# Rows of 320 columns, a tile for the gate matrix, and the later steps' gate sums spread over units 0 to 5

## The chip, the cores and the metric

The kernel runs on one core of one Trainium2 chip. The metric is device time in microseconds of one execution.

## The reference

Three layers follow one another, all in float32.

```python
# 1. attention: 4 x 8 heads, 768 steps, head size 40
for t in range(S):
    m_new = np.maximum(f_gate[:, :, t] + m, i_gate[:, :, t])
    f_stab = np.exp(f_gate[:, :, t] + m - m_new)
    i_stab = np.exp(i_gate[:, :, t] - m_new)
    m = m_new
    C = f_stab * C + i_stab * einsum('bhd,bhe->bhde', vt, kt)
    n = f_stab * n + i_stab * kt
    h_tilde = einsum('bhde,bhe->bhd', C, qt)
    denom = np.maximum(np.abs(einsum('bhd,bhd->bh', n, qt)), 1.0)
    y[:, :, t] = sigmoid(o_gate[:, :, t]) * h_tilde / denom
# 2. experts: 3072 tokens of 320; (token, expert) pairs taken in order of their logit,
#    each expert takes at most 384 tokens, each token one expert
logits = x @ w_gate                       # 8 experts
out[mask_e] = np.maximum(x[mask_e] @ w1[e], 0.0) @ w2[e]      # 320 -> 1024 -> 320
# 3. one dense layer for all tokens
h = x @ w_in                              # 320 -> 2048
out = np.where(h > 0, h, np.exp(np.minimum(h, 0)) - 1) @ w_out
```

## The kernel before

**Attention** (`Attention`) cuts the 768 steps into 12 blocks of 64. A unit u holds block u // 2 and one of two pairs of batches, with eight heads in two halves of the partitions, so there are 24 units, and `run` goes through them in order. All instructions stand in the order in which the Python issues them; each engine's queue, and that of each DMA issuer, takes them in that order.

Ahead of the units the gates are summed up over time, for all 32 (batch, head) pairs at once on 32 partitions: `maximum` is the running m (L227, a scan on DVE), `logs` turns the gates into sums (L236 to L242: two subtractions or additions, a scan, two more), and `split` cuts each sum into three bfloat16 parts `fp` and `pb` (ACT copies at L251 and L252, DVE subtractions at L254 and L255) and copies `pb` twice into `fb` (L258). For the first 128 steps all of it is done in the setup. For the 640 others `maximum` and `logs` are issued in the setup as one piece each, and `split` in three pieces in units 0, 1 and 2, each behind the unit's first matmuls and ahead of `decay`.

A unit u issues, in this order: a warm-up matmul (`idle`, L351); `values(u)` (weights P times v, L360) mixed with `scores(u + 2)` (L292); `decay(u + 2)`, which builds the decay factors with matmuls on `fp` and `fb` (L307 to L317) and takes exponentials on ACT into `db` (L305) and W (L312); `turn(u - 1)`, three transposes of the finished rows x (L431) and a copy on ACT into xT (L433); in units 5, 9, 13, 17 and 21 `tokens`, a transpose of collected logits (L453); `recall(u)` and `state(u)` (L374, L387); `factors` and `fade` on POOL (qt L324, kt L333, C L335); `weigh(u + 1)` on DVE, which writes P (L345); `load_qk(u + 5)` on SP; `opens` on ACT; `gates(u)`, a short chain on DVE (rd, L407 to L411) with the rows x at its end (DVE L414, POOL L415); `logits(u - 1)` (L443 or L445); `add_state` on DVE (L398); `rows_out(u)`; `load_vk(u + 4)` on SP. Between these, `fl` issues pieces of two other jobs: five pieces of the weights' conversion per unit from unit 2 on (a DMA into `cx`, ACT, three DVE operations L894, L898, L901 into cF, ACT `wih` L955, POOL `wil` L957), and tables for the router on DVE from unit 3 on.

A row x is 320 wide and its tile 384: `rows_out` copies columns 256 to 320 once more into 320 to 384 on ACT (L422) and then writes both halves on SP into `xd`, a table of 3072 rows of 384 in device memory. The duplicate serves the later matmuls, which take the last 64 columns twice, once on each half of the partitions. `wg`, the gate matrix, lies in columns 128 to 224 of the tile `keep`, whose first 32 partitions hold the scan's mask; its load is therefore issued on SP behind `logs` (L218).

**Routing and experts.** `Router.round(r)` picks the tokens of one expert at a time, on DVE and PE; `Mlp` does experts and dense layer in eight rounds of 384 tokens. `get_x` gathers a round's rows from `xd` with three indirect DMAs on POOL into `xg`; `prep_x` transposes them (L1078) and splits them into `xh` (ACT) and `xl` (DVE, L1086); `up` does the first products (L1125). In round 0 these steps follow at once; in later rounds a planner (`Plan`, which adds up estimated times by engine) decides when a side job such as `prep_xs` may issue its next instructions between the main matmuls: 5,000 ns of planned time behind `get_x`, and not before the round before is far enough.

Of the kernel before, what the change touches and what calls it, by code (L numbers as in the profile page):

```python
# [17 lines left out]
NS, NU = 12, 24  # L18
# [101 lines left out]
class Attention:  # L120
# [4 lines left out]
    def __init__(self, nc, tc, consts, qk, vk, ig, fg, wg, xd, L, ident):  # L125
        self.nc, self.tc, self.qk, self.vk, self.xd, self.L, self.ident = nc, tc, qk, vk, xd, L, ident
        self.es = ExitStack()
        one = self.es.enter_context(tc.tile_pool(name="a1", bufs=1))
        self.two = self.es.enter_context(tc.tile_pool(name="a2", bufs=2))
        self.psX = self.es.enter_context(tc.tile_pool(name="psX", bufs=1, space=PS))  # L130
        V, G, A = nc.vector, nc.gpsimd, nc.scalar
        self.st = {}
        self.extra = []
        gi = one.tile([32, S], F32, name="gi")
        gf = one.tile([32, S], F32, name="gf")
        nc.sync.dma_start(gf, fg)
        A.dma_start(gi, ig)
        junk = self.psum("pF", 1)
        wz = self.wz = one.tile([128, 512], BF, name="wz")
        V.memset(wz, 0.0)  # L140

        def spin(n):

            for _ in range(n):
                nc.tensor.matmul(junk, wz[:, :128], wz, start=True, stop=True)

        spin(SPIN)
        warm = one.tile([1, 8], F32, name="warm")
        V.memset(warm, 0.0)
        A.activation(warm, warm, AF.Tanh)  # L150
        self.QKb = [one.tile([128, 2, 8, 64], F32, name=f"qk{i}") for i in range(4)]
        self.QK, self.VK, self.W = {}, {}, {}
        for u in range(2):
            self.load_qk(u)
        for u in range(2):
            self.load_vk(u)
        for u in range(2, 4):
            self.load_qk(u)
        for u in range(2, 4):
            self.load_vk(u)  # L160
        m = one.tile([32, S + 1], F32, name="m")
        V.memset(m[:, 0:1], -1e30)
        keep = keep_all = one.tile([128, S], F32, name="keep")
        self.lT, keep = keep[:, :128], keep[:32]
        self.wg = keep_all[:, 128:224].rearrange("p (k e) -> p k e", e=32)
        G.memset(keep, 1.0)
        G.memset(keep[:, 0:S:64], 0.0)
        ac = one.tile([32, S], F32, name="ac")
        i3 = one.tile([96, 32], BF, name="i3")
        for k in range(3):  # L170
            V.tensor_copy(i3[k * 32:k * 32 + 32], ident[:32, :32])
        self.half = one.tile([96, 2], F32, name="half")
        V.tensor_reduce(self.half, i3.rearrange("p (r m) -> p r m", r=2), AX, ALU.max)
        pair = one.tile([96, 16], BF, name="pair")
        V.tensor_tensor(pair, i3[:, :16], i3[:, 16:], op=ALU.add)
        self.sel = one.tile([96, 16, 2, 64], BF, name="sel")
        V.tensor_copy(self.sel, i3.rearrange("p (r m) -> p m r", r=2)[:, :, :, None].to_broadcast([96, 16, 2, 64]))
        self.one_m = one.tile([96, 16, 64], BF, name="one_m")
        A.activation(self.one_m, pair[:, :, None].to_broadcast([96, 16, 64]), AF.Copy)
        self.idb = one.tile([128, 128], BF, name="idb")  # L180
        A.activation(self.idb, ident, AF.Copy)
        low = one.tile([128, 64], BF, name="low")
        G.memset(low, 0.0)
        for r in (0, 64):
            G.affine_select(out=low[r:r + 64], in_=low[r:r + 64], pattern=[[1, 64]], compare_op=ALU.is_ge, fill=-1e30,
                            base=0, channel_multiplier=-1)
        self.low = one.tile([128, 8, 64], BF, name="low8")
        A.activation(self.low, low[:, None].to_broadcast([128, 8, 64]), AF.Copy)
        self.fp = one.tile([96, S], BF, name="fp")
        self.pb = one.tile([96, S], BF, name="pb")  # L190
        self.fb = one.tile([96, NS, 2, 64], BF, name="fb")
        self.CS = [[one.tile([128, 8, 64], F32, name=f"C{b}{i}") for i in range(3)] for b in range(2)]
        for x in self.CS[0] + self.CS[1]:
            G.memset(x[:, :, 41:], 0.0)
        self.KT = [one.tile([128, 512 + 64 - D], F32, name=f"kt{i}") for i in range(2)]
        for x in self.KT:
            G.memset(x, 0.0)
        self.pC = self.psum("pC", 1)
        self.pX = self.psum("pX", 1).rearrange("p h t -> p (h t)")
        self.g = gi, gf, m, keep, ac  # L200

        t0, t1 = slice(0, 128), slice(128, S)
        self.maximum(0, 128)
        self.logs(0, 2)
        for _ in self.split(0, 2):
            pass
        self.opens(0)
        self.both(self.scores(0))
        self.load_qk(4)
        self.decay(0)  # L210
        self.maximum(128, S)
        V.memset(self.pC, 0.0)
        self.decay(1)
        self.both(self.scores(1))
        self.weigh(0)
        self.fade(0)
        self.logs(2, NS)
        nc.sync.dma_start(self.wg, wg)  # L218

    def psum(self, name, bufs):  # L220
        return self.psX.tile([128, 8, 64], F32, name=name, bufs=bufs)
# [6 lines left out]
                                              op1=ALU.max)  # L228

    def logs(self, n0, n1):  # L230

        gi, gf, m, keep, ac = self.g
        V = self.nc.vector
        a, b = n0 * 64, n1 * 64
        t = slice(a, b)
        V.tensor_tensor(gf[:, t], gf[:, t], m[:, t], op=ALU.add)  # L236
        V.tensor_tensor(gf[:, t], gf[:, t], m[:, a + 1:b + 1], op=ALU.subtract)
        if n0 == 0:
            V.memset(gf[:, 0:1], 0.0)
        V.tensor_tensor_scan(ac[:, t], keep[:, t], gf[:, t], 0.0, op0=ALU.mult, op1=ALU.add)  # L240
        V.tensor_tensor(gi[:, t], gi[:, t], m[:, a + 1:b + 1], op=ALU.subtract)
        V.tensor_tensor(gi[:, t], gi[:, t], ac[:, t], op=ALU.subtract)  # L242

    def split(self, n0, n1):

# [156 lines left out]
    def gates(self, u, fl):  # L402

        V = self.nc.vector
        nq = self.st["O", u][:, :, 40]
        rd = self.two.tile([128, 2, 8], F32, name="rd")
        V.tensor_scalar(rd[:, 0], nq, -2.0, 2.0, op0=ALU.mult, op1=ALU.max)  # L407
        fl(1)
        V.scalar_tensor_tensor(rd[:, 0], nq, 2.0, rd[:, 0], op0=ALU.mult, op1=ALU.max)
        fl(5)  # L410
        V.reciprocal(rd[:, 1], rd[:, 0])  # L411
        x = self.st["x", u] = self.two.tile([128, 384], F32, name="x", bufs=3)
        xh = x[:, :320].rearrange("p (h d) -> p h d", d=40)
        V.scalar_tensor_tensor(xh, self.st.pop(("sg", u)), 1.0, self.st.pop(("O", u))[:, :, :40], op0=ALU.add, op1=ALU.mult)  # L414
        self.nc.gpsimd.tensor_tensor(xh, xh, rd[:, 1, :, None].to_broadcast([128, 8, 40]), op=ALU.mult)  # L415

    def rows_out(self, u):
# [1 line left out]
        nc = self.nc  # L419
        n, bp = divmod(u, 2)  # L420
        x = self.st["x", u]
        nc.scalar.activation(x[:, 320:], x[:, 256:320], AF.Copy)  # L422
        for r in range(2):
            row = (bp * 2 + 1 - r) * S + n * 64
            nc.sync.dma_start(self.xd[row:row + 64], x[r * 64:r * 64 + 64])
# [1 line left out]
    def turn(self, u):  # L427
        x = self.st.pop(("x", u))
        p = self.pX
        for k in range(3):  # L430
            self.nc.tensor.transpose(p[:, k * 128:k * 128 + 128], x[:, k * 128:k * 128 + 128], self.ident)  # L431
        xT = self.st["xT", u] = self.two.tile([128, 3, 128], F32, name="xT")
        self.nc.scalar.activation(xT.rearrange("p k t -> p (k t)"), p[:, :384], AF.Copy)  # L433

# [24 lines left out]
            self.extra.pop(0)  # L459

    def run(self, hook, fill):
        later = self.split(2, NS)
        for u in range(NU):
            v, w = u + 1, u + 2
            fl = lambda i: ([fill() for _ in range(FP[i])] if u > FU else []) + [self.step() for _ in range(EP[i])]
            self.idle(u)
            self.both(self.values(u), self.scores(w))
            if u < 3:
                next(later, None)
            if w < NU:  # L470
                self.decay(w)
            if u > 0:
# [12 lines left out]
            if v < NU:  # L485
                self.fade(v)
            self.gates(u, fl)
            fl(2)
            if u > 0:
                self.logits(u - 1)  # L490
# [6 lines left out]
            if u + 4 < NU:  # L497
                self.load_vk(u + 4)
            fl(4)
            hook(u)  # L500
        self.turn(u)
        self.logits(u)
# [338 lines left out]
class Mlp:  # L841
# [209 lines left out]
    def get_x(self, r):  # L1051
        idx = self.router.res[r][1]
        self.xg = []
        for k in range(3):
            t = self.pool.tile([128, 384], F32, name="xg", bufs=3)
            self.xg.append(t)
            self.gather(t, self.xd, idx[:, k:k + 1])

    def psum(self):

# [3 lines left out]
    def spin(self, n):  # L1064

        for _ in range(n):
            self.nc.tensor.matmul(self.junk, self.wih[:, 0, :128], self.wih[:, 0, :512], start=True, stop=True)

    def prep_x(self, r):

        nc, plan = self.nc, self.plan
# [3 lines left out]

        def turn(k):
            for t in range(3):
                nc.tensor.transpose(ps[k][0][:, t * 128:t * 128 + 128], self.xg[k][:, t * 128:t * 128 + 128], self.ident)  # L1078

        def split(k):  # L1080
# [262 lines left out]
    def prep_xs(self):  # L1343

        for r in range(1, NR):
            while self.routed < r:
                yield self.plan.t + 1, ""
            self.get_x(r)
            yield self.plan.t + RX, ""
            while self.prog < r - 1:  # L1350
                yield self.plan.t + 1, ""
            yield from self.prep_x(r)
# [84 lines left out]
def kernel(ctx, tc, qk, vk, ig, fg, wg, w1a, w1b, w2a, win, wout, out):  # L1437
# [5 lines left out]
    ident = consts.tile([128, 128], F32, name="ident")  # L1443
    make_identity(nc, ident)
    L = consts.tile([128, 8, 24], F32, name="L")
    xd = dram.tile([3072, 384], F32, name="xd")
    rt = Router.__new__(Router)
    plan = Plan()
    m = Mlp(nc, tc, consts, w1a, w1b, w2a, win, wout, xd, out, ident, rt, plan)
# [98 lines left out]
```

## Time and profile before

| | |
|---|---|
| median of 3 runs | 772.03 us (771.68 to 773.65) |
| profiled execution: its own time, its span | 776.35 us, 774.5 us |
| busy, share of the span: PE, DVE, ACT, POOL | 92%, 70%, 49%, 28% |
| matmuls on PE | 7384 |
| instruction queue q8 | 58 packets, 0.95 MB |
| DMA in all | 68.89 MB, mean 89 GB/s |

PE is TensorE, DVE VectorE, ACT ScalarE, POOL GpSimd, SP the engine that issues most DMAs. A row of the timeline gives the start in us from the span's start, the duration in us, engine, line, operation, what it writes and reads, and in brackets how long the engine had sat idle and what ended that. "issue" there is a wait for nothing that the profile names.

### The profile page before, as it was taken

Reading aid. Unit: us, or ns where it says so; the run is one execution under the profiler, and the core shown is the slowest. Engines: PE = TensorE matmul, PEld = TensorE weight load, DVE = VectorE, ACT = ScalarE, POOL = GpSimd, SP = SyncE. Lnnn points to the kernel's source line nnn. Section 1 sums busy time; section 2 is a strip of 40 time slices with the busy share of each in tenths; the row PEclk is TensorE's granted clock in tenths of the full one; section 3 lists DMA queues with packets and bytes.
Section 4 is the critical chain, followed back from the end, with each engine's and each line's share of the span. In section 5 each row is a group of like instructions: output and inputs, shape, how many; then the busy total and the mean of one; then the engine's idle time right before and its main releaser. Section 6 shows DMA issues by size and latency. Waiting matters only on the chain.

```text
span 774.5 us, 18272 instructions
## 1 busy us (share of the span) xinstructions
PE 711.0 (92%) x7384; PEld 646.8 (84%) x7384; DVE 543.5 (70%) x1599; ACT 381.6 (49%) x807; POOL 214.9 (28%) x264
## 2 busy tenths in 40 slices
PE   7887887962899999999999999999999999999994
PEld 4565665651799998999999899999999999999994
DVE  8495867758878887885797589669768834842541
ACT  5654544523536644652574277246527734742542
POOL 5687866525401410401121030112023220001001
PEclk9898999885899999999999999999999999999998
DMA  7676867433500410410140032023003321100000
GB/s 258 198 248 193 244 199 222 134 88 105 177 2 2 146 60 1 125 57 27 33 148 20 7 104 78 26 83 99 1 26 111 127 79 36 36 1 25 1 1 26
DMA packets 22820, 68.89 MB, mean 89 GB/s; under 512 B 3536, under 2 KB 7632, under 8 KB 22736
## 3 DMA queue, kind: packets, MB, share of 16 engines
q1 hardware_dynamic: 14240, 35.91, 15.2%
q0 software_dynamic: 8448, 31.73, 12.3%
q8 instruction: 58, 0.95, 0.5%
q14 instruction: 26, 0.21, 0.1%
q10 hardware_dynamic: 48, 0.10, 0.0%
HBM read 59.06 MB, written 8.65 MB: 87 GB/s over the span
## 4 chain that ended last, share of the span: by engine, by line
PE 56%; issue 21%; DVE 8%; POOL 7%; ACT 3%; DMA 3%; SPq 0%; POOLq 0%; DVEq 0%; ACTq 0%
PE ph L1125 25%; PE acc L1264 5%; PE acc L1268 5%; PE acc L1265 5%; PE acc L1232 3%; PE acc L1233 2%; PE acc L1234 2%; POOL qt L324 2%; POOL kt L333 1%; PE acc L1219 1%; POOL x L415 1%; PE pO L374 1%; PE acc L1221 1%; POOL C L335 1%; DVE e L1178 1%
## 5 line engine op out<-in xcount | busy, mean ns | idle before, releaser
L1178 DVE SCALAR_TENSOR_TENSOR e<-e,ph 128x384 f32<-128x384 f32 x128 | 70.4, 551 | 54.7 <-ACT e L1175 54.0
L1174 ACT ACTIVATE e<-ph 128x384 f32<-128x384 f32 x128 | 62.4, 488 | 85.2 <-PE ph L1125 77.6
L1125 PE MATMUL ph<-yh,wih 128*128 128x384 f32 x256 | 89.9, 351 | 0.3
L1142 ACT ACTIVATE gh<-ph 128x384 fp32r<-128x384 f32 x64 | 31.4, 491 | 112.7 <-PE ph L1125 88.6
L1125 PE MATMUL ph<-yh,wil 128*128 128x384 f32 x256 | 86.6, 338 | 0.0
L1274 POOL DMA_INDIRECT out_dram<-ot,idx x24 | 24.1, 1004 | 210.1 <-ACT ot L1002 207.1
L1009 DVE TENSOR_TENSOR gl<-e,gh 128x384 fp32r<-128x384 f32 x128 | 71.1, 562 | 1.7 <-ACT gh L1002 0.3
L1175 ACT ACTIVATE e<-e 128x384 f32<-128x384 f32 x128 | 67.3, 526 | 4.0
L1264 PE MATMUL acc<-woh,gh 128*128 128x320 f32 x216 | 68.2, 316 | 0.0
L1149 DVE SCALAR_TENSOR_TENSOR gl<-ph,gh 128x384 fp32r<-128x384 f32 x64 | 35.3, 554 | 46.8 <-ACT gh L1142 46.4
L1265 PE MATMUL acc<-wol,gh 128*128 128x320 f32 x216 | 66.8, 309 | 0.0
L1268 PE MATMUL acc<-woh,gl 128*128 128x320 f32 x216 | 66.8, 309 | 0.0
L1125 PE MATMUL ph<-yl,wih 128*128 128x384 f32 x256 | 66.6, 342 | 0.0
L1013 POOL DMA_INDIRECT stg<-in_w1a_dram,wi x16 | 15.7, 982 | 148.4 <-DVE wi L782 134.1
L1002 ACT ACTIVATE gh<-e 128x384 fp32r<-128x384 f32 x97 | 49.4, 514 | 11.1 <-DVE e L1178 10.8
L1268 PE MATMUL acc<-woa,gl 128*128 128x320 f32 x168 | 52.4, 312 | 0.8 <-DVE gl L1009 0.8
L1264 PE MATMUL acc<-woa,gh 128*128 128x320 f32 x168 | 53.2, 316 | 0.0
L1265 PE MATMUL acc<-wob,gh 128*128 128x320 f32 x168 | 52.0, 309 | 0.0
L1125 PEld LDWEIGHTS ph<-yh,wih 128*128 128x128 f32 x256 | 48.3, 189 | 4.1 <-ACT yh L1237 4.1
L1125 PEld LDWEIGHTS ph<-yh,wil 128*128 128x128 f32 x256 | 48.2, 188 | 0.0
L1125 PEld LDWEIGHTS ph<-yl,wih 128*128 128x128 f32 x256 | 46.2, 188 | 0.0
L1125 PE MATMUL ph<-xh,w1h 128*128 128x384 f32 x128 | 44.9, 350 | 0.0
(275 smaller groups left out, 2096.6 us busy)
## 6 DMA issues: line engine op xcount, KB each, us to landing
vk<-in_vk_dram SPq DMA_DIRECT2D x24, 484.0 KB, 4.4
qk<-in_qk_dram SPq DMA_DIRECT2D x20, 320.0 KB, 5.0
xd<-x SPq DMA_DIRECT2D x48, 96.0 KB, 2.7
cx<-in_win_dram SPq DMA_DIRECT2D x8, 512.0 KB, 6.1
wx<-in_wout_dram SPq DMA_DIRECT2D x9, 320.0 KB, 3.0
cx<-in_wout_dram SPq DMA_DIRECT2D x5, 448.0 KB, 6.0
qk<-in_qk_dram SPq DMA_DIRECT2D x4, 512.0 KB, 6.7
cx<-in_win_dram SPq DMA_DIRECT2D x4, 256.0 KB, 6.0
```

Of the source, the lines that this page charges most:

```text
L1002: self.nc.scalar.activation(out, x, AF.Copy)
L1009: self.nc.vector.tensor_tensor(out, x, y, op=ALU.subtract)
L1125: PE.matmul(p, w, x, start=k == 0, stop=k == 7)
L1142: nc.scalar.activation(h, p, AF.Relu)
L1149: nc.vector.scalar_tensor_tensor(l, p, 0.0, h, op0=ALU.max, op1=ALU.subtract)
L1174: nc.scalar.activation(e, p, AF.Relu, scale=-1.0)
L1175: nc.scalar.activation(e, e, AF.Exp, scale=-1.0)
L1178: nc.vector.scalar_tensor_tensor(e, e, -1.0, p, op0=ALU.add, op1=ALU.max)
L1264: PE.matmul(p, h[:, c], wh, start=f == 0, stop=False)
L1265: PE.matmul(p, h[:, c], wl, start=False, stop=False)
L1268: PE.matmul(p, l[:, c], wh, start=False, stop=f == 15)
L1274: s = nc.gpsimd.indirect_dma_start(out=self.out, out_offset=bass.IndirectOffsetOnAxis(ap=idx[:, t:t + 1], axis=0), in_=o, in_offset=None)
```

## The change

Four things change. The rows are 320 wide in the tile x and in `xd`; the copy of the last 64 columns leaves `rows_out` and is made in the second part by `twice`, three times a round, on ACT, behind the gather; the third transpose in `turn` takes 64 columns, and pX is cleared once. The gate matrix has its own tile and is loaded early. `maximum` and `logs` for the later steps are done in two parts, steps 128 to 256 and 256 to 768, by `behind`, a generator whose next piece is issued twice a unit: behind `gates` and at the unit's end. `split` goes with it, so its pieces no longer stand ahead of `decay`. Counted out, unit 0 gets `logs(2, 4)` and the first piece of `split(2, 4)`, unit 1 the rest of it, unit 2 `maximum(256, S)` and the first two operations of the sums, unit 3 the scan and the last two, unit 4 two pieces of `split(4, NS)` and unit 5 the last.

```diff
         for u in range(2, 4):
             self.load_qk(u)
+        self.wg = one.tile([128, 3, 32], F32, name="wg")
+        nc.sync.dma_start(self.wg, wg)
         for u in range(2, 4):
             self.load_vk(u)
...
-        self.wg = keep_all[:, 128:224].rearrange("p (k e) -> p k e", e=32)
...
-        self.maximum(128, S)
+        self.maximum(128, 256)
         V.memset(self.pC, 0.0)
+        V.memset(self.pX, 0.0)
...
-        self.logs(2, NS)
-        nc.sync.dma_start(self.wg, wg)
...
+    def behind(self):
+        self.logs(2, 4)
+        yield
+        yield from self.split(2, 4)
+        yield
+        self.maximum(256, S)
+        yield
+        yield from self.steps(4, NS)
+        yield from self.split(4, NS)
+
+    def steps(self, n0, n1):
...
         V.tensor_tensor(gf[:, t], gf[:, t], m[:, t], op=ALU.add)
         V.tensor_tensor(gf[:, t], gf[:, t], m[:, a + 1:b + 1], op=ALU.subtract)
+        yield
...
         V.tensor_tensor_scan(ac[:, t], keep[:, t], gf[:, t], 0.0, op0=ALU.mult, op1=ALU.add)
+        yield
         V.tensor_tensor(gi[:, t], gi[:, t], m[:, a + 1:b + 1], op=ALU.subtract)
         V.tensor_tensor(gi[:, t], gi[:, t], ac[:, t], op=ALU.subtract)
+        yield
...
-        x = self.st["x", u] = self.two.tile([128, 384], F32, name="x", bufs=3)
+        x = self.st["x", u] = self.two.tile([128, 320], F32, name="x", bufs=3)
...
-        nc.scalar.activation(x[:, 320:], x[:, 256:320], AF.Copy)
...
-            self.nc.tensor.transpose(p[:, k * 128:k * 128 + 128], x[:, k * 128:k * 128 + 128], self.ident)
+            z = 128 if k < 2 else 64
+            self.nc.tensor.transpose(p[:z, k * 128:k * 128 + 128], x[:, k * 128:k * 128 + z], self.ident)
...
     def run(self, hook, fill):
-        later = self.split(2, NS)
+        later = self.behind()
...
-            if u < 3:
-                next(later, None)
...
             self.gates(u, fl)
+            next(later, None)
...
             fl(4)
+            next(later, None)
...
-            self.gather(t, self.xd, idx[:, k:k + 1])
+            self.gather(t[:, :320], self.xd, idx[:, k:k + 1])
...
+    def twice(self, k, ns=256):
+        self.nc.scalar.activation(self.xg[k][:, 320:], self.xg[k][:, 256:320], AF.Copy)
+        if ns:
+            self.plan.on("a", ns)
...
         def turn(k):
             for t in range(3):
+                if (r, t) == (0, 0):
+                    self.twice(k, 0)
...
             self.get_x(r)
             yield self.plan.t + RX, ""
+            for k in range(3):
+                self.twice(k)
+            yield self.plan.t, "a"
...
-    xd = dram.tile([3072, 384], F32, name="xd")
+    xd = dram.tile([3072, 320], F32, name="xd")
```

## Rows read from the trace of the kernel before

**Rows 1.** PE's busy tenths in 40 equal slices of the span.
```profile
PE   7887887962899999999999999999999999999994
```
**Rows 2.** Busy us by stretch: length, PE, PEld, DVE, ACT, POOL; clock, DMA, GB/s.
```profile
60.00:70.00 10.00, 6.50 (x132) 4.50 (x126) 5.12 (x11) 2.23 (x6) 6.16 (x7) 0.66 0.47 150
...
400.00:500.00 100.00, 99.95 (x681) 95.15 (x680) 76.42 (x249) 50.77 (x108) 14.27 (x19) 1.00 0.16 51
```
**Rows 3.** Timeline, PE: the warm-up matmuls of units 1 to 6.
```profile
16.52 0.39 PE L351 MATMUL pO<-wz 128*128 128x512 bf16 x1
...
23.70 0.39 PE L351 MATMUL pO<-wz 128*128 128x512 bf16 x1
...
32.99 0.61 PE L351 MATMUL pO<-wz 128*128 128x512 bf16 x1
...
38.40 0.39 PE L351 MATMUL pO<-wz 128*128 128x512 bf16 x1
...
45.39 0.39 PE L351 MATMUL pO<-wz 128*128 128x512 bf16 x1
...
51.19 0.39 PE L351 MATMUL pO<-wz 128*128 128x512 bf16 x1
```
**Rows 4.** Timeline, PE: two waits.
```profile
17.97 0.33 PE L360 MATMUL pO<-vk,P 64*64 64x64 f32 x3 [1.07 <-DVE P L345]
...
63.64 0.26 PE L387 MATMUL pC<-vk,kt 64*64 64x64 f32 x1 [3.50 <-issue]
```
**Rows 5.** Busy time by stretch, columns as in Rows 2.
```profile
20.00:37.50 17.50, 14.20 (x356) 10.51 (x351) 8.24 (x18) 11.46 (x23) 10.94 (x11) 0.80 0.67 195
37.50:57.50 20.00, 16.67 (x524) 12.16 (x519) 18.59 (x43) 10.43 (x24) 16.64 (x17) 1.00 0.80 249
```
**Rows 6.** Timeline, DVE: first and last of the sums, three waits, P.
```profile
10.29 0.91 DVE L236 TENSOR_TENSOR gf<-gf,m 32x640 f32<-32x640 f32 x1
...
14.31 1.36 DVE L242 TENSOR_TENSOR gi<-gi,ac 32x640 f32<-32x640 f32 x1
...
27.10 0.83 DVE L894 TENSOR_SCALAR cF<-cx 128x512 int32<-128x512 int32 x1 [1.86 <-DMA cx<-in_win_dram]
...
31.62 0.17 DVE L407 TENSOR_SCALAR rd<-pO 128x8 f32<-128x8 f32 x1 [3.68 <-PE pC L387]
...
37.69 0.17 DVE L407 TENSOR_SCALAR rd<-pO 128x8 f32<-128x8 f32 x1 [3.03 <-PE pC L387]
...
48.86 0.68 DVE L345 TENSOR_TENSOR P<-pS,W 128x512 f32<-128x512 f32 x1
```
**Rows 7.** A line's instructions: durations in ns least, median, most; first and last start; shapes.
```profile
L254 DVE TENSOR_TENSOR ac<-ac,fp x4: 279/546/823, 6.2 to 20.7; 32x128 f32<-32x128 f32 x2, 32x640 f32<-32x640 f32 x2
...
L227 DVE TENSOR_TENSOR_SCAN m<-gf,m,gi x2: 463/998/1533, 3.9 to 7.4; 32x128 f32<-32x128 f32 x1, 32x640 f32<-32x640 f32 x1
```
**Rows 8.** Timeline: POOL and DVE at work together.
```profile
20.78 1.32 POOL L333 TENSOR_TENSOR kt<-vk,W 128x320 f32<-128x320 f32 x1
...
21.60 1.17 DVE L255 TENSOR_TENSOR gi<-gi,pb 32x640 f32<-32x640 f32 x1
```
**Rows 9.** Timeline, ACT and PE in unit 21.
```profile
152.86 0.26 ACT L422 ACTIVATE x<-x 128x64 f32<-128x64 f32 x1 [1.25 <-POOL x L415]
...
154.53 0.33 PE L453 MATMUL pX<-ident,keep 128*128 128x128 f32 x1 [1.02 <-ACT xT L433]
```
**Rows 10.** Waits up to 168 us: total us, times, longest.
```profile
PE pX L453 <- ACT xT L433: 4.0, 5, 1.0
```
**Rows 11.** Timeline, PE: rounds 0 and 1 of the second part.
```profile
200.26 0.84 PE L1078 MATMUL ph<-ident,xg 128*128 128x128 f32 x3
...
275.38 0.62 PE L1125 MATMUL ph<-xl,w1h 128*128 128x384 f32 x2 [0.69 <-DVE xl L1086]
```
**Rows 12.** Busy time up to two of PE's pauses, columns as in Rows 2.
```profile
0.00:60.20 60.20, 49.00 (x1241) 34.92 (x1242) 46.53 (x101) 34.93 (x73) 41.33 (x71) 0.91 0.75 237
...
0.00:99.60 99.60, 80.96 (x2134) 58.28 (x2134) 74.45 (x158) 53.14 (x113) 71.52 (x99) 0.90 0.74 229
```

More of the change, by code (lines that the diff above doesn't have):

```diff
@@ L162, in __init__ @@
         V.memset(m[:, 0:1], -1e30)
-        keep = keep_all = one.tile([128, S], F32, name="keep")
+        keep = one.tile([128, S], F32, name="keep")
         self.lT, keep = keep[:, :128], keep[:32]
-        self.wg = keep_all[:, 128:224].rearrange("p (k e) -> p k e", e=32)
         G.memset(keep, 1.0)
@@ L230, in logs @@
     def logs(self, n0, n1):
+        for _ in self.steps(n0, n1):
+            pass
+    def behind(self):
[8 more added lines that the diff above has]
+    def steps(self, n0, n1):
         gi, gf, m, keep, ac = self.g
```

## The prediction

> **What bounds the kernel now.** I read first when PE is busy, then the busy shares by stage, and only then the waits, because an average hides two programs in one. PE is at nine tenths or more in every slice from about 213 us on but the last [rows 1], and busy 99.95 us of 100 between 400 and 500, at full clock [rows 2]: nothing there gets shorter unless matmuls are removed, and the change removes none. Ahead of that, up to 168 us, runs attention. Its slices stand at 7 to 9 tenths, and between 60 and 70 us PE is busy 6.50 us of ten at a clock of 0.66, with DMA at 0.47. The slice at 2 tenths behind it is the first routing round, a chain on DVE that the change leaves alone. Since PE is full later, each microsecond by which attention ends earlier is one of the whole, and the question is what attention's 24 units wait for.
>
> The start of each unit is its warm-up matmul [rows 3]. Unit 3 takes 38.40 - 32.99 = 5.41 us, which I use as the length of a unit that nothing holds up for long. Unit 1 takes 23.70 - 16.52 = 7.18 and unit 2 32.99 - 23.70 = 9.29. PE's own waits [rows 4] tell two kinds apart. In unit 1 it waits 1.07 us for P, a named piece of work. In unit 7, at 63.64, it waits 3.50 us for nothing that the profile names. At the start of unit 3 the warm-up takes 0.61 us where it takes 0.39 in others: TensorE is at 1.2 GHz there, after the stalls of unit 2.
>
> DVE is the other engine to read here [rows 5]: from 20 to 37.5 us it is busy 8.24 of 17.5, from 37.5 to 57.5 it is busy 18.59 of 20. So the idle time in units 1 and 2 sits directly in front of a stretch in which DVE is full.
>
> **The early units.** In the kernel before, the five DVE operations of the gates' sums over 640 columns run from 10.29 to 15.67 us in one piece [rows 6], and the split's first subtractions behind them, all ahead of P of unit 1: that is the 1.07 us. ACT's copies of 640 columns stand ahead of db, W and xT in units 1 and 2 in the same way. The change does 128 columns there, at 0.28 us an operation and 0.46 for the scan where 640 take 0.82 and 1.53 [rows 7], and moves the other 512 behind. Units 1 and 2 should then take about 5.4 each: 7.18 + 9.29 - 10.8 = 5.7 us earlier at the start of unit 3.
>
> **What the moved work costs where it goes.** Between the 128 and 640 columns of rows 7 I interpolate 512: 0.28 + 0.75 x 0.54 = 0.69 us for a two-input operation and 0.46 + 0.75 x 1.07 = 1.26 for a scan. Moved to units 2, 3 and 4 are two scans and eight two-input operations, 2.5 + 5.5 = 8.0 us. From the start of unit 2 to that of unit 5, 23.70 to 45.39 [rows 3], DVE idles 1.86 + 3.68 + 3.03 = 8.6 us [rows 6] and so works 13.1. Now unit 2 starts at 23.70 - 1.8 = 21.9, DVE owes 13.1 + 8.0 = 21.1, and the 1.86 us for the first weights' DMA remain: 44.9 us at the start of unit 5, against 45.39. If PE had to follow DVE closely, only 0.5 us of the 5.7 would be left. It needn't quite: P of unit 6 is ready at 48.86 + 0.68 = 49.54 [rows 6], and unit 6 starts at 51.19, so DVE may fall 1.65 us further behind before this holds PE. The lead that survives lies between 0.5 and 2.2 by that; I take 2.1, near the upper end, because the stalls of PE that gave DVE its idle time had PE at the low clock as well. The bounds are 0 and the whole 5.7.
>
> ACT's moved copies, in units 4 and 5, stand on an engine that is busy 10.43 of 20 us there [rows 5] and come at nothing; in a row without that cover, the last four can put an xT back by a microsecond. Clearing pX (DVE, 512 columns) comes ahead of the first P, in the microsecond that the shorter first scan gives back (1.53 against 0.46), and costs its half microsecond only without it.
>
> One row speaks against even that lead. At 21.60 a subtraction over 640 columns took 1.17 us beside a POOL operation of 1.32 us that runs up to 22.10 [rows 8]; that of rows 7 took 0.82 at most. The Trainium skill has a rule for it (GPSIMD Engine Reference, Key points): GpSimd shares its SBUF interfaces with VectorE and contends with instructions that read two SBUF inputs. By that rule the moved operations, nearly all with two SBUF inputs, come into a stretch in which POOL works 16.64 of 20 us [rows 5]. The trace agrees in this pair; were all 8.0 us stretched by 1.17/0.82, they would cost 3.4 us more, which is more than the lead that I leave, and this is what the first rival does.
>
> **The copy of 64 columns.** It leaves every unit, 24 times 0.26 us on ACT [rows 9]. What counts is its place: it waits for POOL's x, and db, W and xT stand behind it. That reaches PE only where PE wants xT at once, in units 5, 9, 13, 17 and 21, which transpose the logits' sums: 4.0 us of waits in 5 [rows 10]. In unit 21 ACT idles 1.25 us ahead of the copy, the copy ends at 153.12, db, W and xT take until PE goes on at 154.53, 0.47 each, and PE has waited 1.02 [rows 9]. Without the copy db would be done in that idle time: 0.5 us less. Five of those are 2.5; in the earlier units ACT also stands behind a DVE that is full, so I take 1.6 (bounds 0 and the 4.0). In other units the matmuls of recall and state, 64 between the transposes and the logits, hide xT; without them these would gain too.
>
> **Three copies a round in the second part.** In round 0 PE's last three transposes start at 200.26 as soon as the last gathered rows are there [rows 11], with the first product behind them; a copy of 0.26 us goes in between: +0.3 (bounds 0 and 0.8, all three). In round 1 PE waits 0.69 us for xl [rows 11]; three copies now go ahead of it on ACT, which may sit there until the third block of rows has landed: +0.4 (bounds 0 and 0.8). In later rounds matmuls of the round before are queued on PE, and I cost them at nothing; without that cover it would be 0.8 a round, 4.8 in six.
>
> **What I cost at nothing.** Rows of 1,280 instead of 1,536 bytes take 32 KB off a unit's writes, 0.13 us at 249 GB/s [rows 5], and these writes are read only after attention. The load of wg no longer holds SP's queue until DVE has done the sums; behind it there stood the keys of unit 5, wanted by unit 3, after 33 us. Now it stands ahead of the values of units 2 and 3, whose use also gets earlier, by its own issue alone; the bound is one issue, a few tenths. The third transpose still moves 128 columns.
>
> **The sum:** -2.1 - 1.6 + 0.3 + 0.4 = -3.0 us. The profiled execution took 776.35 us, its span being 774.5; that makes 773.35. The median shown is 4.3 lower, 772.03, and against it the forecast is 769.0. Under 0.3%, 2.3 us, a change can't be told from none, so this is just beyond it.
>
> **Rivals.** *Everything is given back on DVE* (the contention above, lead 0): what remains is -1.1 for the copies, since DVE then delays xT in the early ones, and +0.7: 771.6 us. For it speaks DVE's full stretch in rows 5; against it the 1.65 us of slack of P.
> *The lead is kept whole*, the moved operations fitting into waits of DVE such as it must have in PE's 3.50 us of unit 7: -5.7 - 1.6 + 0.7 = -6.6, 765.4 us. Against it: unit 7 comes after the full stretch.
> *Slower: more pauses of PE at its code.* The pause of 3.50 us comes after 1241 matmuls and another, at 99.6, after 2134 [rows 12]: 893 apart, 7 times 127.6. The execution's 7384 matmuls over the 58 packets of one instruction queue are 127.3 a packet. So PE seems to outrun its code while DMA engines are full. Earlier units mean denser loads, and so more or longer pauses. This decides from 5.3 us of added pauses on; two more of 3.50 make -3.0 + 7.0 = +4.0, 776.0 us. Against it: such pauses come in few of the units, and units 1 and 2 only get as fast as unit 3. (The Trainium skill, Runtime: NRT & Kernel Launch, Instruction fetch mechanics, has the crossing of such a block mostly hidden; by it this rival would cost nothing, and the trace, with its 3.50 us, does not agree.)
>
> **Numbers.** Forecast 0.46 (own range 767 to 771), given back 0.22, kept 0.16, slower 0.16. Of the forecast's chance two thirds, 0.30, lie beyond 0.3%, the rest within: faster 0.30 + 0.16 = 0.46, same 0.16 + 0.22 = 0.38, slower 0.16. The range, 764.5 to 774.5, takes in the first two rivals and stops short of the third's middle.
>
> **What would show it.** The profile after should have unit 3 start near 27 us, DVE full from about 25 us on, and the lead shrunk to 1 to 3 us by unit 6; the five waits for xT nearer 0.5 than 1 us; and the first product of the second part 0.3 us further behind the last gather. It would be wrong if the pauses at the code move: one more or one less is as large as the sum.

## The result, and the profile after

The changed kernel takes 778.48 us in the median of four runs (775.35 to 785.29), against 772.08 for the kernel before on the same chip (771.68 to 773.65): a ratio of 1.010, interval [1.0058, 1.0142]. A ratio here isn't the quotient of the two medians (that would be 1.008), and it leaves out runs of more than 1.5% above the fastest of their kernel. Forecast were 769.0 us with faster as the likeliest; it is slower, beyond the range of 764.5 to 774.5. The profiled execution of after is one of its short ones, 775.5 us with a span of 773.7, and that of before one of its long ones (776.35). So the two profiles, laid side by side, don't show the 6 us as a difference of spans. What they show is where the lead of the first units went.

First the page of after: busy tenths of PE and DVE in 40 slices of the span, and the granted clock of TensorE.

```profile
PE   7778787953999999999999999999999999999994
...
DVE  7898777868878877885797689569858834842541
...
PEclk9989999975899999999999999999999999999998
```

PE's row behind the routing round is that of [rows 1]: nothing has changed there. The stretches of [rows 5] and [rows 2] in the kernel after (length, PE, PEld, DVE, ACT, POOL; clock, DMA, GB/s):

```profile
20.00:37.50 17.50, 14.38 (x429) 10.63 (x425) 13.89 (x30) 8.04 (x20) 10.45 (x10) 1.00 0.69 195
37.50:57.50 20.00, 13.43 (x331) 9.77 (x334) 19.55 (x32) 11.89 (x24) 13.95 (x12) 0.83 0.59 179
60.00:70.00 10.00, 8.22 (x292) 6.12 (x282) 9.94 (x19) 5.39 (x12) 8.55 (x9) 1.00 0.68 223
400.00:500.00 100.00, 99.95 (x680) 95.13 (x679) 76.66 (x256) 50.10 (x109) 14.33 (x19) 1.00 0.14 45
```

From 20 to 37.5 us PE issues 429 matmuls where [rows 5] have 356, at full clock instead of 0.80: that is the lead. From 37.5 to 57.5 it issues 331 where [rows 5] have 524. DVE is busy 19.55 of 20 us there, and 9.94 of 10 between 60 and 70, where [rows 2] have 5.12. The lead is not merely used up, it is overdrawn. The starts of units 4 to 7 say the same (PE's timeline, the warm-up matmuls):

```profile
34.52 0.39 PE L369 MATMUL pO<-wz 128*128 128x512 bf16 x1
...
44.98 0.61 PE L369 MATMUL pO<-wz 128*128 128x512 bf16 x1
...
52.34 0.39 PE L369 MATMUL pO<-wz 128*128 128x512 bf16 x1
...
59.24 0.39 PE L369 MATMUL pO<-wz 128*128 128x512 bf16 x1
```

Against [rows 3] unit 4 starts 38.40 - 34.52 = 3.9 us sooner, unit 5 by 0.4, unit 6 by 1.15 later; unit 7 comes 59.24 - 56.59 = 2.65 later than in the kernel before (PE's timeline):

```profile
56.59 0.39 PE L351 MATMUL pO<-wz 128*128 128x512 bf16 x1
```

Single profiles differ here: unit 7 starts at 55.63 when the kernel before runs again and at 61.82 when the changed one does, so its delay has the same sign in each pair, but not the same size.

Most of the lead goes in unit 4, which takes 44.98 - 34.52 = 10.46 us against 45.39 - 38.40 = 6.99. PE waits there for unit 3's rows x from POOL and for C from DVE, 3.0 us together (PE's timeline, the wait in brackets, then POOL's and DVE's):

```profile
38.66 0.55 PE L449 MATMUL pX<-ident,x 128*128 128x128 f32 x3 [1.65 <-POOL x L433]
...
40.81 0.37 PE L405 MATMUL pC<-vk,kt 64*64 64x64 f32 x2 [1.35 <-DVE C L416]
```

```profile
37.03 1.57 POOL L433 TENSOR_TENSOR x<-x,rd 128x320 f32<-128x320 f32 x1 [0.62 <-PE pF L328]
38.57 1.70 POOL L342 TENSOR_TENSOR qt<-qk,db 128x512 f32<-128x512 f32 x1
```

```profile
36.88 1.20 DVE L256 TENSOR_TENSOR_SCAN ac<-keep,gf 32x512 f32<-32x512 f32 x1
38.01 1.13 DVE L916 SCALAR_TENSOR_TENSOR cF<-cx,cF 128x512 int32<-128x512 int32 x1
39.08 1.28 DVE L581 TENSOR_SCALAR tblt<-tblt 128x128 int32<-128x128 int32 x1
40.28 0.48 DVE L416 TENSOR_TENSOR C<-C,pC 128x328 f32<-128x328 f32 x1
```

The moved scan comes just behind DVE's part of x and ahead of C. POOL's x beside it takes 1.57 us (0.72 at 55.73), and C starts only behind the scan and two longer operations. Behind these two waits TensorE is granted 0.50 of its clock, that is 1.2 GHz, from 40.8 to 45.0 us, where the kernel before has 2.4 GHz (1.00) through its unit 4. That kernel waits 0.21 us at this transpose, not for C, and 1.78 us for xT, for which the changed one waits 0.64. `after_again` has 2.26 us for x and 1.34 for C, `sums_only` (below) 2.26 and 1.27.

Unit 5 starts at 44.98 where the forecast's sum for DVE had 44.9. The rest goes behind that. DVE's timeline in this stretch:

```profile
31.34 0.67 DVE L251 TENSOR_TENSOR gf<-gf,m 32x512 f32<-32x512 f32 x1
32.04 1.64 DVE L252 TENSOR_TENSOR gf<-gf,m 32x512 f32<-32x512 f32 x1
...
42.44 1.67 DVE L259 TENSOR_TENSOR gi<-gi,ac 32x512 f32<-32x512 f32 x1
...
46.08 0.67 DVE L272 TENSOR_TENSOR ac<-ac,fp 32x512 f32<-32x512 f32 x1
46.68 1.20 DVE L273 TENSOR_TENSOR gi<-gi,pb 32x512 f32<-32x512 f32 x1
...
52.42 1.75 DVE L273 TENSOR_TENSOR gi<-gi,pb 32x512 f32<-32x512 f32 x1
54.10 0.67 DVE L363 TENSOR_TENSOR P<-pS,W 128x512 f32<-128x512 f32 x1
```

The P at 54.10 is unit 6's; [rows 6] have it at 48.86. Of the ten moved operations four, the subtractions of `split(4, NS)`, ran only behind the start of unit 5, in front of this P. And operations of one shape take either 0.67 us or up to 1.75. POOL's timeline beside them tells which:

```profile
31.74 1.40 POOL L975 TENSOR_TENSOR wil<-cF,wih 128x512 fp32r<-128x512 f32 x1 [1.28 <-ACT wih L973]
...
42.10 1.47 POOL L975 TENSOR_TENSOR wil<-cF,wih 128x512 fp32r<-128x512 f32 x1 [1.83 <-ACT wih L973]
...
46.25 1.10 POOL L433 TENSOR_TENSOR x<-x,rd 128x320 f32<-128x320 f32 x1 [0.83 <-DVE x L432]
...
52.34 1.29 POOL L975 TENSOR_TENSOR wil<-cF,wih 128x512 fp32r<-128x512 f32 x1 [1.29 <-ACT wih L973]
```

Each long one lies across a POOL operation and ends 0.54 us behind that one's end (33.68 against 33.14, 44.11 against 43.57, 54.17 against 53.63); the one at 46.68 ends at 47.88, 0.53 us behind POOL's. All ten moved ones sum to 11.4 us, of which the scans make 1.27 and 1.20, against 8.0 in the forecast. PE waits for the late P (PE's timeline, the wait in brackets):

```profile
50.09 0.33 PE L471 MATMUL pX<-ident,keep 128*128 128x128 f32 x1 [1.32 <-ACT xT L451]
...
54.83 0.27 PE L378 MATMUL pO<-vk,P 64*64 64x64 f32 x2 [2.11 <-DVE P L363]
```

The first of these waits comes from the moved copies on ACT. They wait for DVE's subtractions (the second one stretched to 1.20 us), and db, W and xT stand behind them (ACT's timeline):

```profile
46.79 0.63 ACT L269 ACTIVATE fp<-ac 32x512 bf16<-32x512 f32 x1 [1.31 <-DVE ac L272]
47.92 0.63 ACT L270 ACTIVATE pb<-gi 32x512 bf16<-32x512 f32 x1 [0.50 <-DVE gi L273]
...
49.54 0.50 ACT L451 ACTIVATE xT<-pX 128x384 f32<-128x384 f32 x1
```

### The profile page after: what moved, and what is told of

It reads as the page before. It is cut to its first block, busy times and chain, and to the rows that moved or that the text cites. A ratio compares the mean times of both kernels' runs of the same rounds, so it can differ in the third digit from the quotient of the medians.

```text
span 773.7 us, 18260 instructions
## 1 busy us (share of the span) xinstructions
PE 707.3 (91%) x7380; PEld 643.1 (83%) x7384; DVE 554.1 (72%) x1611; ACT 380.9 (49%) x814; POOL 219.2 (28%) x264
## 4 chain that ended last, share of the span: by engine, by line
PE 66%; issue 12%; POOL 7%; DVE 7%; DMA 4%; ACT 2%; SPq 0%; POOLq 0%; another core or an unknown queue 0%; DVEq 0%; ACTq 0%
PE ph L1150 31%; PE acc L1289 6%; PE acc L1293 6%; PE acc L1290 6%; PE acc L1257 3%; DMA qk<-in_qk_dram 2%; PE acc L1259 2%; PE acc L1258 2%; POOL qt L342 2%; PE acc L1244 1%; POOL kt L351 1%; PE acc L1246 1%; POOL x L433 1%; PE ph L1103 1%; PE pr L762 1%
## 5 line engine op out<-in xcount | busy, mean ns | idle before, releaser
L1020 ACT ACTIVATE gh<-e 128x384 fp32r<-128x384 f32 x96 | 49.0, 514 | 11.4 <-DVE e L1203 11.1
L1031 POOL DMA_INDIRECT stg<-in_w1a_dram,wi x16 | 15.7, 982 | 122.5 <-DVE wi L800 118.2
```

The source lines that it names most:

```text
L1020: self.nc.scalar.activation(out, x, AF.Copy)
```

## The experiments

Ratios are to the kernel before on the same chip, with the 95% interval. Its median in the three groups was 771.41, 772.34 and 772.92 us, and its single runs reached from 767 to 780: these are effects of half a per cent inside a spread of one and a half.

**The two kernels again.** No edit, so that the rest has a base.

> The kernel before once more, for a second profile. If the median gap of 6.4 us comes from PE's pauses at blocks of its code, this profile should show fewer or shorter pauses than the first one of before (3.50, 2.93, 2.02, 1.78, 1.65 us), because the first ran 4.3 us above the median: a time near 772 us and pauses that sum to about 8 us. If the gap comes from fixed costs, the pauses of the two profiles of before should agree within 1 us and so should the times.

> The changed kernel once more. All theories expect a median of 776 to 781 us. Theory 'sums on DVE': unit 7 starts 2 to 3 us later than in the kernel before (59.24 against 56.59 us in the first profiles), whatever the total. Theory 'pauses': the starts of the units differ from those of its first profile by several us, at places where PE waits for nothing named. Theory 'copies': attention ends as early as in the first profile, and the second part is longer than before by 2 us or more.

The kernel before against itself: 772.96 us, 0.9978 [0.9942, 1.0014]. The kernel after: 775.39 us (768.98 to 781.38 in 12 runs), 1.0034 [0.9999, 1.0069]. Slower again, by less than in the first four runs, and this interval by itself just reaches 1; the two results together put the loss between a third of a per cent and one. Two expectations were missed. In the second profile of the kernel before, PE's waits for nothing that the profile names sum to 13.2 us against 11.9 in the first, not to about 8, though its span is 2.9 us shorter. And unit 7 of the changed kernel comes 5 to 6 us later in this pair of profiles, not 2 to 3.

**One half at a time.** `sums_only` keeps rows of 384 and the copy in attention; it takes only the gates' sums in two parts, with the gate matrix in its own tile (two small constant tiles share the P tile's room). `rows_only` does the opposite.

```diff
 sums_only, against after
...
-        x = ... self.two.tile([128, 320], F32, name="x", bufs=3)
+        x = ... self.two.tile([128, 384], F32, name="x", bufs=3)
...
+        nc.scalar.activation(x[:, 320:], x[:, 256:320], AF.Copy)
...
-    def twice(self, k, ns=256):
...
 rows_only, against before
-        x = ... self.two.tile([128, 384], F32, name="x", bufs=3)
+        x = ... self.two.tile([128, 320], F32, name="x", bufs=3)
...
-        nc.scalar.activation(x[:, 320:], x[:, 256:320], AF.Copy)
...
+    def twice(self, k, ns=256):
...
```

> Only the gate sums in two parts and the gate matrix in its own tile; rows stay 384 wide with the copy in attention. (Two small setup buffers share P's ring, to make room.) Theory 'sums on DVE': it carries the slowdown, 775 to 780 us, unit 7 starting 2 us or more behind before. Theory 'copies': as before, 771 to 773 us.

> Only the rows of 320 and the three copies a round in the second part; the gate sums stay as before. Theory 'copies': it carries the slowdown, 775 to 779 us. Theory 'sums on DVE': 770 to 773 us, the 0.5 us less at the five transposes of logits in attention, and 1 to 2 us more in the second part.

`sums_only` took 777.4 us, 1.0065 [1.0036, 1.0094]; `rows_only` 772.02, 0.9995 [0.9964, 1.0025]. The loss goes with the sums; what the rows cost or gain can't be told from nothing. `sums_only` also shows the lead at its full size before it goes (PE's timeline, units 2 to 4, and the wait for P of unit 6):

```profile
21.66 0.39 PE L368 MATMUL pO<-wz 128*128 128x512 bf16 x1
...
26.67 0.39 PE L368 MATMUL pO<-wz 128*128 128x512 bf16 x1
...
32.74 0.39 PE L368 MATMUL pO<-wz 128*128 128x512 bf16 x1
...
53.62 0.27 PE L377 MATMUL pO<-vk,P 64*64 64x64 f32 x2 [1.82 <-DVE P L362]
```

Unit 3 at 26.67 against 32.99 in [rows 3], a lead of 6.3 us where 5.7 were forecast; unit 7 at 59.6 against 56.59.

**Load on DVE alone.** Two kernels leave the kernel before as it is and put operations that nobody needs in the slots of units 2 to 4, behind `gates` and at the unit's end. They write over gate values (`gf`) that have been used by then.

```diff
+    def extra_work(self, u):
+        t = slice(256, S)
+        if 2 <= u <= 4:
 dve_two_in
+            for _ in range(2):
+                V.tensor_tensor(gf[:, t], gf[:, t], m[:, t], op=ALU.subtract)
 dve_no_in
+            for _ in range(3):
+                V.memset(gf[:, t], 0.0)
```

> The kernel before, with two extra DVE subtractions of 32 x 512 (two SBUF inputs, on tiles that nothing reads any more) behind the gates and at the end of units 2, 3 and 4: twelve in all, 12 x 0.68 = 8.2 us of DVE work by itself, as much as the change moves there. Nothing is taken out of units 0 and 1. Theory 'DVE and POOL shut each other out': half or more of the twelve take 1.2 us or longer, unit 7 starts 8 to 11 us later than in the kernel before (about 64 to 66 us), and the time is 778 to 784 us. Theory 'plain DVE time': all take 0.68, unit 7 starts 4 to 6 us later, 775 to 778 us. If DVE is not the bound, no change.

> The same at the same places with eighteen fills of 32 x 512 that read nothing, 18 x 0.48 = 8.6 us of DVE work. Theory 'shut out': the fills keep their 0.48 us beside POOL, so this costs clearly less than the two-input operations: unit 7 starts 3 to 6 us later, 774 to 778 us. Theory 'plain DVE time': the same as the two-input operations within 1 us.

`dve_two_in` 777.57 us, 1.0082 [1.005, 1.0114]; `dve_no_in` 777.46, 1.0045 [1.0015, 1.0075]. The 18 clears, which read nothing, took the same 0.485 us each, 16 of them beside a POOL operation; the 12 subtractions took 0.67 to 1.67, five of them over 1 us (a line's instructions, one view of each kernel: least, median, most):

```profile
L250 DVE MEMSET gf<- x18: 485/485/485, 33.4 to 55.0; 32x512 f32 x18
```

```profile
L250 DVE TENSOR_TENSOR gf<-gf,m x12: 671/676/1673, 33.1 to 57.1; 32x512 f32<-32x512 f32 x12
```

By its sums of busy time 8.7 us of clears were added and 11.3 of subtractions, which are 8.1 (12 x 0.676) where POOL is quiet. So 8.7 us of work that isn't held up in this way cost 0.45% (3.5 us), and 11.3 cost 0.82% (6.3 us). Time on DVE in units 2 to 4 costs by itself, roughly 0.4 to 0.6 us of the whole for each. Being shut out by POOL makes the same operations longer; that this adds to the time is not shown, since the intervals overlap and the medians are level, 5.1 and 5.2 us above 772.34. Only the starts of unit 7 set the two apart, 64.4 us in `dve_two_in` and 61.0 in `dve_no_in`. Neither theory for `dve_two_in` came out whole: two of twelve subtractions took 1.2 us or more, not half, and unit 7 came 7.8 us later than in the kernel before, more than plain time on DVE was to cost and just less than the other theory had. The pair in `dve_two_in` that starts at 46.59 shows the shutting out (DVE's timeline, then POOL's; x2 are two operations in one row):

```profile
46.59 2.36 DVE L250 TENSOR_TENSOR gf<-gf,m 32x512 f32<-32x512 f32 x2
```

```profile
46.95 1.45 POOL L967 TENSOR_TENSOR wil<-cF,wih 128x512 fp32r<-128x512 f32 x1 [2.43 <-ACT wih L965]
```

**The sums earlier, or the conversions later.** `sums_early` is the kernel after with `maximum` for all steps ahead of the loop, as before, and `steps(4, NS)` run beside `split(2, 4)` in units 0 and 1, `split(4, NS)` in 2 and 3. `fill_later` leaves the sums and begins the conversion of the second part's weights (cF, wih, wil) in unit 6 instead of 2, six pieces a unit instead of five.

```diff
 sums_early, against after
-        self.maximum(128, 256)
+        self.maximum(128, S)
...
         self.logs(2, 4)
         yield
-        yield from self.split(2, 4)
-        yield
-        self.maximum(256, S)
-        yield
-        yield from self.steps(4, NS)
+        (split(2, 4) and steps(4, NS) in turns, three slots)
         yield from self.split(4, NS)
 fill_later, against after
-FP = [1, 1, 1, 1, 1, 0]
+FP = [1, 1, 1, 1, 1, 1]
-FU = 1
+FU = 5
```

> The changed kernel with the later sums three slots earlier: the scan of m for all steps in the setup as before, the three pieces of the sums from 256 on in units 0 and 1 beside the split of 128 to 256, and the split from 256 on in units 2 and 3. The instructions are the same but for the length of two scans. Theory 'shut out in units 2 to 4': most of the loss goes, P of unit 6 at 47 to 50 us instead of 53 to 57, 769 to 773 us. Theory 'pauses': no better than the change, 775 to 778 us.

> The changed kernel with the conversion of the dense layer's weights (three DVE operations and one of POOL for each piece) started in unit 6 instead of 2, six pieces of it a unit instead of five. Theory 'shut out': with some 2 us of DVE and 1 us of POOL a unit gone, the early lead stays: unit 7 starts at 50 to 54 us (59 to 62 with the change), and the end gains what the later units can still take in, 766 to 774 us. Theory 'ACT or the gate matrix's load': unit 7 still starts 2 us or more behind the kernel before.

`sums_early` 772.61 us, 1.0011 [0.9981, 1.0041]; `fill_later` 774.28, 1.0025 [0.9994, 1.0055]. `sums_early` takes the loss away; `fill_later` lies between, by less than its uncertainty from either end. In `sums_early` P of unit 6 starts at 49.1 us again and unit 7 at 57.8, though DVE is no less full (stretches as above):

```profile
20.00:37.50 17.50, 13.01 (x351) 9.31 (x350) 16.15 (x28) 10.88 (x25) 9.75 (x8) 0.98 0.61 177
37.50:57.50 20.00, 15.60 (x470) 11.64 (x469) 18.78 (x44) 11.73 (x24) 17.00 (x17) 0.94 0.78 242
```

The same operations stand where DVE had idle time, up to 37.5 us, and PE gets 470 matmuls into the second stretch instead of 331. `fill_later` missed its expectation for the starts: unit 3 at 32.4 and unit 7 at 59.0 us. DVE was no longer full (busy 10.0 us of the 17.5 up to 37.5, and 16.2 of the next 20); PE paused at its code three times in the first units (PE's timeline):

```profile
17.93 0.27 PE L378 MATMUL pO<-vk,P 64*64 64x64 f32 x2 [2.02 <-issue]
```

with 1.56 us more at 24.53 and 2.58 at 30.45.

**Two controls, and a try at something better.** `sums_early_again` is `sums_early` once more. `before_fill` moves the conversions in the kernel before as `fill_later` did in the one after. `early_fill` begins them in unit 4 (FU = 3, six pieces) on top of `sums_early`.

> The same kernel as sums_early, timed again, since 1.0011 [0.9981, 1.0041] doesn't settle whether it gives back the change's loss or also gains. If the loss of the change lies in the slots of units 2 to 5 and rows of 320 columns are worth nothing, it lies on the kernel before: 0.998 to 1.002. If the lead of units 1 and 2 is kept once the sums are out of the way, part of the 5.7 us of it show: 0.993 to 0.997. Its first product of the second part at 194 us, as in its first profile, speaks for the second; at 198 to 201 us, where the kernel before has it, for the first.

> The kernel before with the conversion of the weights moved from unit 2 on to unit 6 on, as fill_later moved it in the kernel after. If fill_later came closer to the kernel before because VectorE has room for the sums once the conversions are away, the move is worth little here, where VectorE is 26 to 27 of 36 us busy between 24 and 60 us anyway: 0.998 to 1.002. If the move of the conversions is a gain by itself, whatever the sums do, it shows here too, by the 0.9 of a per cent by which fill_later lies below the kernel with the sums moved alone: 0.990 to 0.996. If they are lacked later on: above 1.003.

> sums_early with the conversion of the weights from unit 4 on (six pieces of it in a unit instead of five). If VectorE's fullness in units 2 to 4 is what keeps the lead of units 1 and 2 from lasting, unit 7 starts at 52 to 56 us (57.8 in sums_early) and the time falls below the kernel before: 0.992 to 0.998. If PE's pauses at the blocks of its code, which come sooner after one another when PE works faster, take up whatever VectorE gives free, unit 7 stays at 57 to 60 us and the ratio at 0.999 to 1.004.

`sums_early_again` 773.21 us, 1.001 [0.9986, 1.0035]: level with the kernel before, and no part of the lead shows in the time. Its first product of the second part starts at 196.6 us, between the two places named beforehand. `before_fill` 776.78, 1.0043 [1.0011, 1.0075]: moving the conversions costs by itself, which neither of the first two readings had. It starts unit 7 early, at 53.3 us, and pays between 60 and 168 us (PE's waits, total, times, longest):

```profile
PE pX L431 <- POOL x L415: 6.0, 7, 1.7
```

There the kernel before has 1.6 us in 2. So `fill_later` must be set against `before_fill`: with the conversions out of the way the changed kernel is not behind the unchanged one (1.0025 against 1.0043, each uncertain by 0.003). `early_fill` 777.03, 1.0047 [1.0018, 1.0076]: its P of unit 6 came at 45.7 us, but unit 7 at 59.5, after pauses of 1.54, 1.56, 1.76 and 2.17 us at its code up to 48 us. No version beats the kernel before beyond its uncertainty.

## Why the prediction was wrong

**The early units: right in `sums_only`, not in every profile.** The wait for P in unit 1 goes when the sums leave the front, and `sums_only` has unit 3 at 26.67 where about 27 was forecast. But `sums_early` and its repeat have it at 29.42 and 28.71, and `after_again` at 31.07, level with the second profile of the kernel before (30.97; the first has 32.99). In after, PE no longer waits 1.07 us for P up to 17.97 as in [rows 4], and stops instead for nothing that the profile names, 1.62 us up to 17.36; `after_again` has such stops of 1.70 and 1.76 us ahead of unit 3.

**The step that failed** is "The lead that survives lies between 0.5 and 2.2". In the runs nothing survives: unit 7 starts 2.65 us later than in the kernel before in the profile of after, 3.0 in `sums_only`, and `sums_only` is slower by 0.65%. Three things in it were wrong.
First, DVE's debt was drawn up to the start of unit 5 as if all ten operations were done by then. Four stand behind it, with 0.67 + 1.20 + 0.68 + 1.75 = 4.3 us, directly in front of P of unit 6. That the sum came out at 44.9 and the trace at 44.98 is therefore no confirmation: less of the moved work was in it, and what was in it took longer.
Second, PE was to be free of DVE by a slack of 1.65 us, read from P of unit 6 alone. PE had to follow DVE sooner, and by other results: in unit 4 it waited 1.65 us for x and 1.35 for C, and only 0.4 us of the lead was left at unit 5. Then P came 5.2 us later than in [rows 6], so that slack was gone too, and PE waited 2.11 us.
Third, the eight two-input operations were priced by [rows 7] alone, whose longest, over 640 columns, is 0.82 us. The contention was seen in [rows 8], sized at 3.4 us and put into a rival; it measured 11.4 - 8.0 = 3.4 us. The rival's mistake was to stop at "lead 0": a debt that arises behind the lead can be larger than it.
The Trainium skill's rule (GPSIMD Engine Reference, Key points), which the forecast weighed, speaks of contention between GpSimd and VectorE instructions in a 2-port performance mode or with two SBUF inputs. The trace agrees for two inputs, with 0.67 us against 1.64 to 1.75, and the clears of `dve_no_in`, which have no input, stay at 0.485.

**What then is the loss?** The sums are 11.4 us of DVE work in a stretch where DVE was already full with attention and the conversions. `dve_two_in` gives the kernel before such a load without moving anything, and a loss of that size; `sums_early` does the same sums sooner and has no loss. These two show the place of the work to be the cause. The gate matrix's early load, which `sums_only` has as well, is in `sums_early` too and so isn't the cause. How much of it is plain time on DVE and how much being shut out stays open between the bounds given above.

**ACT's copies at nothing: wrong.** The text named the cover and what it costs without it, a microsecond. The copies waited for the subtractions, one of them stretched, and PE's wait for xT in unit 5 is 1.32 us where the kernel before has 0.74.

**The copy of 64 columns: mis-sized.** 1.6 us were taken. The five waits for xT did not shrink to 0.5 each (PE's waits up to 168 us, in after; [rows 10] before):

```profile
PE pX L471 <- ACT xT L451: 4.3, 5, 1.3
```

In `rows_only`, where the sums don't disturb them, they are 3.6 us, the longest 0.7. So some 0.4 us came instead of 1.6, which the time of `rows_only`, 0.9995 [0.9964, 1.0025], can't contradict or confirm.

**The copies in the second part: mis-sized.** 0.3 us were taken for round 0 and 0.4 for round 1. Round 0 costs more than all three copies together were thought to be able to (0.8). From its first transposes to its first product the profiles with rows of 384 take 2.9 to 4.0 us (mean 3.6, six profiles), those with 320 take 4.0 to 5.0 (mean 4.7, seven): 1.1 us more. In after, each copy stands on ACT behind the `xh` of the block of rows before it, so the blocks follow one another (ACT's timeline):

```profile
195.67 0.49 ACT L1120 ACTIVATE xh<-ph 128x384 fp32r<-128x384 f32 x1 [0.57 <-PE ph L1103]
196.06 0.25 ACT L1088 ACTIVATE xg<-xg 128x64 f32<-128x64 f32 x1
```

From the first product to the end of the span, profiles with rows of 384 take 572.3 to 573.1 us (mean 572.7), those with 320 take 572.8 to 574.5 (mean 573.3): 0.6 us more, about the spread within a group. It can't be put down to single waits. Round 1's 0.69 us of [rows 11] is gone; in round 2 a wait for xl of 0.31 to 0.43 us is new in all seven, so "cover by the round before" did not hold fully there, and one of 0.87 us for a copy stands in the profile of after alone (PE's timeline):

```profile
328.63 0.33 PE L1103 MATMUL ph<-ident,xg 128*128 128x128 f32 x1 [0.87 <-ACT xg L1088]
...
331.88 0.45 PE L1150 MATMUL ph<-yh,wih 128*128 128x384 f32 x1 [0.43 <-DVE xl L1111]
```

Together that is 1.7 us where 0.7 was forecast. With the 0.4 us of the copy in attention the rows would then lose 1.3 us, an estimate from these profiles; `rows_only` allows it, since its interval ends at 1.0025.

The same sums tell where nearly all the spread of the profiles comes from. The last part differs by 2 us among the thirteen, while the first product starts anywhere from 194.2 (`sums_early`) to 205.7 us (`after_again`). What comes ahead of it sets the time.

**The third rival, pauses at the code.** PE's waits of over 0.6 us for nothing that the profile names, up to 165 us, sum to 11.9 in the kernel before, 13.2 when it ran again, 12.8 in after, 14.5 in `after_again`, 11.2 in `sums_only`, 11.4 in `dve_two_in`, 8.7 in `before_fill` and 15.7 in `early_fill`. Many come after the same counts of matmuls in kernel after kernel (1241 and 2134, as in [rows 12], and 1879; four less in after, whose trace lacks some records); that loading code is their cause is inferred from this spacing, not shown. Their sums don't go with the ratios (`dve_two_in` and `before_fill` have few and are slower), so they are not the cause of the loss. They are part of why a lead isn't kept: `fill_later` and `early_fill` lost theirs in them, and after has 3.4 us of them by 33 us, where the kernel before has none up to 60 us.

## What to carry to other kernels

Work that leaves a stall must be followed to the place where it lands: draw up the receiving engine's idle time there as a list of gaps, and put every moved operation, with its real place in the order, in front of the next result that the bounding engine wants. Price a VectorE operation with two SBUF inputs from a row in which GpSimd works as it will beside it; here that was up to 1.75 instead of 0.67 us, and 1.12 in the mean of the eight. A slack has to be read for every result that the bounding engine takes from the filled one (here x, C and P), not for one of them. And a rival with the right price must be carried through to its end: "the gain is given back" has no floor at nothing.

## What the runs showed of the hardware

In this kernel VectorE's operations with both inputs in SBUF and GpSimd's operations keep each other out almost wholly. The plainest case is in unit 0 of after, where a subtraction over 128 columns, 0.28 us in [rows 7], took 3.50 (DVE's timeline, then POOL's):

```profile
14.23 3.50 DVE L252 TENSOR_TENSOR gf<-gf,m 32x128 f32<-32x128 f32 x1
```

```profile
14.27 0.73 POOL L351 TENSOR_TENSOR kt<-vk,W 128x320 f32<-128x320 f32 x1
14.96 0.71 POOL L433 TENSOR_TENSOR x<-x,rd 128x320 f32<-128x320 f32 x1
15.64 1.25 POOL L342 TENSOR_TENSOR qt<-qk,db 128x512 f32<-128x512 f32 x1
16.86 0.72 POOL L351 TENSOR_TENSOR kt<-vk,W 128x320 f32<-128x320 f32 x1
```

Four POOL operations ran back to back, to 17.58, and the subtraction ended at 17.73: it waited for a gap.

Two inputs aren't needed for that. The `TENSOR_SCALAR` of 128 columns at 39.08 above, which reads one tile, took 1.28 us and ended 0.09 us behind POOL's operation (40.36 against 40.27); one of this shape took 0.23 in the kernel before while POOL was idle (DVE's timeline):

```profile
38.78 0.23 DVE L561 TENSOR_SCALAR tblt<-jt 128x128 int32<-128x128 int32 x1
```

Not held up were the clears of `dve_no_in` and P, whose operand pS lies in PSUM: at 44.04 in after it took 0.67 us, with POOL at work from 43.51 to 45.41.

It goes the other way too: POOL's x, 0.71 us here, took 1.25 on average in the same kernel between 24 and 60 us, where the kernel before has 0.88.
